# Four engines' order lists rewritten: a GpSimd addition ahead of the W1 load's issue, a ScalarE reciprocal ahead of a relu, and a new order around layer two's last phi(K) tiles

## The chip, the core and the metric

The kernel runs on one core of one Trainium2 chip. A core has five engines that run their own instruction queues in order: TensorE (PE in the profile, with PEld for its weight loads), VectorE (DVE), ScalarE (ACT), GpSimd (POOL) and SyncE (SP, which here only issues DMAs). They meet through semaphores. The metric is the device time of one execution in microseconds (us), the median over several runs; lower is better.

## The reference, cut to what matters

Four residual blocks follow each other on x of 2048 tokens by 512 channels, bf16 in and out: linear attention, MLP, linear attention, MLP. Both layers use the same weights.

```python
def A(x, wqkv, wo):                  # 32 heads of 16 channels
    q, k, v = split(x @ wqkv)
    phi = lambda t: where(t > 0, t + 1, exp(t)) + 1e-6
    pq, pk = phi(q), phi(k)
    kv = einsum("bhsd,bhse->bhde", pk, v)       # sum over all tokens
    z  = einsum("bhsd->bhd", pk)                # sum over all tokens
    o  = (pq @ kv) / ((pq . z) + 1e-6)
    return o @ wo
def B(x, w1, b1, w2, b2):                        # F = 1792
    return gelu(layernorm(x) @ w1 + b1) @ w2 + b2
x = x + A(layernorm(x)); x = x + B(layernorm(x))   # layer one
x = x + A(layernorm(x)); x = x + B(layernorm(x))   # layer two
```

The sums over all tokens in `kv` and `z` are what matters here: no attention output of a layer can be made before the last token tile of that layer has passed through phi(K).

## The kernel before

**Tiles.** Tokens are cut into 16 tiles of 128 (numbered 0 to 15) and four chunks of four tiles (0 to 3). Weights stay in SBUF. In the names, the first number is the layer counted from 0, so `K1_14` is layer two.

**An attention block.** For each token tile the row is normalised (`stats`, `aggr`, `veps`, `pow`, `norm`), transposed (by PE as `PT`, by DMA as `TA`, `TB`) and multiplied with Wk (`K`, L860). `phi` (L823 to 849) then makes phi(K) in three or four instructions: an exponential on ACT (`expk`, L830), a relu on ACT (`reluk`, L841), a minimum on DVE (`mink`, L834 or L843) and the sum on DVE or POOL (`phik`, L847), or instead of relu and sum one fused DVE instruction that reads PSUM (`phik`, L836). Q goes the same way (`Q` L878 or L891, `expq`, `reluq`, `minq`, `phiq`). V is never formed: `G` (L961, L993) accumulates y-transposed times phi(K), and `KV` (L1016) multiplies that with Wv. `z` is summed per chunk by PE (`Z`, L942) or, for the first three chunks of layer two, in fp32 on POOL and DVE (`za`, L914), split in a high and a low half by `zhi` (L920) and `zlo` (L923) and summed over tokens by `ZH` (L930).

**From the sums to the output.** `KV` goes through a mask (`kvm`, L1035) and is multiplied with Wo (`M`, L1039), copied to bf16 (`cpm`, L977 on DVE or L974 on ACT), and used in `WO` (L1109), whose result is added to x (`RA`, L1114). The denominator is made in one of two ways. By channel: `D` (L1085), then ln and exp(-ln) on ACT (`ln` L1087, `rec` L1089) and a product on DVE or POOL (`pr`, L1093). By token: product with a row of z (`pz`, L1061), a sum per head (`red`, L1064), `den` (L1067), `rec` (L1069), `pr` (L1073), and a DMA transpose (`TP`, L1077).

**The MLP.** `W1` (L1141) with gelu on ACT (L1147), `W2` (L1180) with the residual on DVE (`RB`, L1186, L1190). The weights W1 and W2 are loaded in two halves each by DMAs that POOL issues (`w1_0`, `w1_1`, `w2_0`, `w2_1`, L682). Both halves of W1 are needed by every `W1` group.

**What sets the order.** Nothing is searched for when the kernel is built. `CONF["ORDER"]` holds for each engine the full list of its instruction groups by name, written out (from L345 on). `Scheduler.run` (L127) walks the five lists, gives each group its buffers and PSUM banks in the order in which its own estimate reaches them, and `assign_waits` (L283) turns the dependences and the reuse of buffers into semaphore waits. `play` (L1305) emits each list in order. Each engine thus runs its list strictly in order, and a group that waits holds everything behind it on its engine. Which buffer a group gets, and so which earlier group it has to wait for, follows from the lists too: there are four `eb` buffers, four `rb` buffers, eight `pkb` buffers, two `lr` buffers and eight PSUM banks.

```python
            queue = {e: [by_name[n] for n in self.named[e].split()] for e in ENGINES}
...
        G.op("act", lambda e, r=r: e.activation(lr[:, r.slot, :], lr[:, r.slot, :], ACT.Exp, scale=-1.0), 536,
             reads=[f"l{tag}"], writes=[f"l{tag}"], tiles=[r], prio=p, name=f"rec{tag}", lat=110, table="exp")
...
        lambda e, kt=kt, r=r: e.tensor_tensor(yTa(pq)[:, kt, :], yTa(pq)[:, kt, :], lr[:, r.slot, :], op=ALU.mult),
...
        G.op("dve", lambda e: e.tensor_tensor(eb[:, zl.slot, :], zacc[:], dz[:], op=ALU.subtract), 600, reads=["zacc", "dz"],
             writes=["zlo"], tiles=[zl], prio=prio, name=f"zlo{L}", lat=60, fast=True)
```

Of the kernel before, what the change touches and what calls it, by code (L numbers as in the profile page):

```python
# [282 lines left out]
def assign_waits(graph, order, sems, dma_sems):  # L283
# [10 lines left out]
    while len(done) < total:  # L294
        moved = False
        for e in ENGINES:
# [117 lines left out]
        "dve":  # L414
# [962 lines left out]
```

## Time and profile before

| what | value |
|---|---|
| median of 3 runs | 326.38 us (326.32 to 327.12) |
| the profiled execution, its own time | 326.46 us |
| its span, first to last instruction | 324.7 us |
| granted TensorE clock over the span | 1.000 |
| HBM read, written | 8.00 MB, 2.10 MB |

A row of a timeline reads: start in us from the start of the span, length in us, engine, source line, operation, output and inputs by the program's names, shapes, and xN where N like instructions in a row are merged. A bracket at the end says how long the engine had been idle and what ended that. The chain of waits lists what ended last, step by step, backwards from the end, printed in order of time. A 512-column matmul is listed with about 0.38 us, but the next one starts 0.216 us after it, so that starts, not lengths, tell how fast PE goes.

### The profile page before, as it was taken

How to read it: one execution, taken by the hardware profiler on the slowest of the kernel's cores; microseconds unless marked ns; L12 is line 12 of the kernel's file. 1: busy time of each engine (PE TensorE's matmuls, PEld its weight loads, DVE VectorE, ACT ScalarE, POOL GpSimd, SP SyncE). 2: the span in 40 equal slices, each digit the busy share in tenths (PEclk: the TensorE clock that was granted, in tenths of full speed). 3: DMA queues.
4: the chain of work that ended last, by engine and by line, in shares of the span. 5: the costliest groups of instructions: out<-in, count | busy, mean ns of one | idle time of the engine just before them, and what ended most of it. 6: DMA issues, size and time to landing. Idle time of an engine off the chain costs nothing.

```text
span 324.7 us, 4792 instructions
## 1 busy us (share of the span) xinstructions
PE 320.7 (99%) x1729; PEld 158.4 (49%) x1729; DVE 218.6 (67%) x506; ACT 195.2 (60%) x336; POOL 134.9 (42%) x224
## 2 busy tenths in 40 slices
PE   8999999999999999999999999999999999999996
PEld 4444544675444444444444444458644444444443
DVE  5997779999985760213759999999999564000232
ACT  6999698773136129488974567869832543576000
POOL 4673276628803259000266735683541754000000
PEclk9999999999999999999999999999999999999999
DMA  7524558112320205310003200022133123000004
GB/s 241 179 43 89 145 166 296 42 38 49 77 52 5 46 16 91 74 32 2 0 0 68 48 16 2 17 50 50 33 67 81 33 51 81 16 0 2 32 27 153
DMA packets 47028, 20.39 MB, mean 63 GB/s; under 512 B 42076, under 2 KB 45532, under 8 KB 47004
## 3 DMA queue, kind: packets, MB, share of 16 engines
q1 hardware_dynamic: 45532, 15.06, 20.2%
q0 software_dynamic: 1056, 4.72, 4.5%
q10 hardware_dynamic: 416, 0.30, 0.3%
q8 instruction: 14, 0.23, 0.3%
q14 instruction: 10, 0.08, 0.1%
HBM read 8.00 MB, written 2.10 MB: 31 GB/s over the span
## 4 chain that ended last, share of the span: by engine, by line
PE 90%; DVE 6%; ACT 2%; DMA 1%; POOL 0%; issue 0%
PE ps L1141 30%; PE ps L1180 28%; PE ps L1109 9%; PE ps L860 7%; PE ps L878 5%; PE ps L993 3%; PE ps L961 3%; PE ps L891 2%; PE ps L1167 1%; DMA t<-in_A_x_dram 1%; DVE eb L843 1%; DVE gtb L977 1%; DVE gacc L1003 1%; DVE yb L782 1%; PE ps L942 1%; PE ps L805 1%
## 5 line engine op out<-in xcount | busy, mean ns | idle before, releaser
L1147 ACT ACTIVATE gT<-ps,b1c 128x512 bf16<-128x512 f32 (+1 forms) x140 | 77.0, 600 | 63.3 <-PE ps L1141 62.6
L1141 PE MATMUL ps<-t,w 128*128 128x512 bf16 (+1 forms) x560 | 101.4, 336 | 0.0
L1180 PE MATMUL ps<-w,gT 128*128 128x512 bf16 x434 | 98.2, 379 | 0.0
L1141 PEld LDWEIGHTS ps<-t,w 128*128 128x128 bf16 x560 | 54.6, 98 | 43.9 <-ACT t L815 0.3
L1180 PEld LDWEIGHTS ps<-w,gT 128*128 128x128 bf16 x434 | 42.5, 98 | 50.0
L757 POOL TENSOR_TENSOR rstd<-veps,neghalf 128x1 f32<-128x1 f32 x64 | 38.7, 616 | 5.3 <-DVE veps L755 3.1
L830 ACT ACTIVATE eb<-ps 128x512 bf16<-128x512 f32 x56 | 32.6, 600 | 12.4 <-PE ps L860 5.5
L1190 DVE TENSOR_TENSOR pkb<-ps,xsb 128x512 bf16<-128x512 f32 x15 | 10.1, 684 | 40.7 <-PE ps L1180 40.7
L742 DVE BATCH_NORM_STATS2 stats<-xsb 128x6 f32<-128x512 f32 x48 | 32.2, 678 | 0.4
L860 PE MATMUL ps<-wqkv,t 128*128 128x512 bf16 x128 | 31.4, 379 | 0.1
L1109 PE MATMUL ps<-gtb,t 128*128 128x512 bf16 x128 | 30.9, 379 | 0.0
L841 ACT ACTIVATE rb<-ps 128x512 bf16<-128x512 f32 x38 | 22.1, 602 | 8.0 <-PE ps L860 6.6
L747 POOL TENSOR_SCALAR veps<-mv 128x1 f32<-128x1 f32 x32 | 8.7, 271 | 43.8 <-DVE mv L744 40.9
L755 POOL TENSOR_SCALAR veps<-mv 128x1 f32<-128x1 f32 x28 | 7.3, 267 | 45.5 <-DVE mv L744 44.0
L777 ACT ACTIVATE yb<-xsb,nmr,rstd 128x512 bf16<-128x512 f32 x21 | 16.9, 809 | 11.7 <-POOL nmr L774 11.7
L782 DVE TENSOR_SCALAR yb<-xsb,mv,rstd 128x512 bf16<-128x512 f32 x27 | 15.7, 590 | 11.9 <-POOL rstd L757 11.7
L1186 DVE TENSOR_TENSOR xsb<-ps,xsb 128x512 f32<-128x512 f32 x16 | 10.9, 682 | 16.5 <-PE ps L1180 16.5
L843 DVE TENSOR_SCALAR eb<-eb 128x512 bf16<-128x512 bf16 x46 | 14.9, 333 | 7.8 <-ACT eb L830 7.6
L878 PE MATMUL ps<-wqkv,t 128*128 128x512 bf16 x80 | 20.1, 379 | 0.0
L860 PEld LDWEIGHTS ps<-wqkv,t 128*128 128x128 bf16 x128 | 12.2, 98 | 15.0 <-ACT t L815 0.5
L1109 PEld LDWEIGHTS ps<-gtb,t 128*128 128x128 bf16 x128 | 12.3, 97 | 14.3 <-ACT gtb L974 0.5
L1126 POOL TENSOR_TENSOR xsb<-xsb,b2b 128x512 f32<-128x512 f32 x14 | 17.3, 1235 | 1.0 <-DVE yb L782 0.7
(103 smaller groups left out, 395.7 us busy)
## 6 DMA issues: line engine op xcount, KB each, us to landing
w<-in_B_w_dram POOLq DMA_DIRECT2D x4, 896.0 KB, 7.2
out_dram<-pkb SPq DMA_DIRECT2D x15, 128.0 KB, 2.0
t<-in_A_x_dram SPq DMA_DIRECT2D x3, 512.0 KB, 6.9
t<-yb SPq DMA_TRANSPOSE x56, 2.5
wqkv<-in_A_wqkv_dram SPq DMA_DIRECT2D x1, 512.0 KB, 5.3
wqkv<-in_A_wqkv_dram POOLq DMA_DIRECT2D x1, 512.0 KB, 4.4
wo<-in_A_wo_dram POOLq DMA_DIRECT2D x1, 512.0 KB, 5.5
t<-t SPq DMA_TRANSPOSE x20, 2.4
```

Source lines behind the costliest of these rows:

```text
L742: G.op("dve", lambda e: e.bn_stats(stats[:, s.slot, :], src()), 602, reads=src_keys, writes=[k + "s"], tiles=[s, *src_tiles], prio=prio, n ...
L757: G.op("pool", lambda e: e.tensor_tensor(rstd[:, s.slot:s.slot + 1], veps[:, s.slot:s.slot + 1], neghalf[:], op=ALU.pow), 530, reads=[k + ...
L782: G.op("dve", lambda e: e.tensor_scalar(yb[:, y.slot, :], src(), stats[:, s.slot, 2:3] if by_act else mv[:, s.slot, 0:1], rstd[:, s.slot:s ...
L830: G.op("act", lambda e: e.activation(eb[:, et.slot, :], bank(bt), ACT.Exp, scale=factor()), 569 if by else 483, reads=[src_key, *more], wr ...
L841: G.op("act", lambda e: e.activation(rb[:, rt.slot, :], bank(bt), ACT.Relu, scale=factor()), 569 if by else 478, reads=[src_key, *more], w ...
L843: G.op("dve", lambda e: e.tensor_scalar(eb[:, et.slot, :], eb[:, et.slot, :], 1.0, 1e-6, op0=ALU.min, op1=ALU.add), 202, reads=[f"e{tag}"] ...
L860: ins = e.matmul(bank(b), lhsT=yTa(yT)[:, dt, k * P:(k + 1) * P], rhs=wqkv[:, dt, D:2 * D], start=(dt == 0), stop=(dt == DT - 1))
L878: ins = e.matmul(bank(b), lhsT=yTa(yT)[:, dt, k * P:(k + 1) * P], rhs=wqkv[:, dt, 0:D], start=(dt == 0), stop=(dt == DT - 1))
L1109: ins = e.matmul(bank(wb), lhsT=yTa(pq)[:, kt, k * P:(k + 1) * P], rhs=gtb[:, kt, :], start=(kt == 0), stop=(kt == DT - 1))
L1141: ins = e.matmul(bank(b, n), lhsT=w1[:, dt, ft * P:(ft + 1) * P], rhs=yTa(yT)[:, dt, k0 * P:k1 * P], start=(dt == 0), stop=(dt == DT - 1))
L1147: G.op("act", lambda e, ft=ft, b=b, k0=k0, k1=k1, n=n: e.activation(gT[:, g.slot, ft * 512 + k0 * P:ft * 512 + k1 * P], bank(b, n), ACT.Ge ...
L1180: ins = e.matmul(bank(b), lhsT=gT[:, g.slot, ft * 512 + k * P:ft * 512 + (k + 1) * P], rhs=w2[:, ft, :], start=(ft == 0), stop=(ft == FT - 1))
```

## The change

Only the lists in `CONF["ORDER"]` change. PE's list is the same, word for word, and no instruction is added, removed or given to another engine.

Layer one:

- ACT: `rec0_0_3` (the reciprocal of the last of four channel blocks of chunk 0) now stands ahead of `reluq0_1_1`, not behind it.
- POOL: `phiq0_1_1` (a sum of 128x512) now stands ahead of `w1_0`, the DMA issue of one half of W1, not behind it.

Layer two, around the end of phi(K) (tiles 10 to 15) and the first Q tiles:

- ACT: within the 43 places behind `expk1_11`, 34 hold another group than before; among them `expq1_1_2` and `reluq1_1_2` move forward, `expk1_13` and `expk1_15` behind their relus, `reluq1_3_1` ahead of `ln1_0_1`, `expq1_3_0` and `reluq1_2_0` directly behind the three `cpm1` copies.
- DVE: within the 78 places behind `normA1_15`, 59 hold another group than before; `ga1_1_0` and `phiq1_1_2` move ahead of `zhi1`, `mink1_15` directly ahead of it, `minq1_0_1` and `minq1_0_2` behind `phik1_14`, `phiq1_1_3` from ahead of `gt1_0` to between the `kvm1` groups, `minq1_3_1` and `minq1_3_0` far back.
- POOL: `phiq1_3_1` ahead of `pr1_1_0`, `vepsB1_0` ahead of `vepsB1_1`.
- SP: the transposes `TP1_1_2` and `TP1_1_3` change places.

Because the lists change, 43 groups of layer two wait for other groups than before (other `eb`, `rb` buffers and PSUM banks).

```diff
 "act":
-            "reluq0_1_1 rec0_0_3 cpz0 ln0_0_2 rec0_0_2 ...
+            "rec0_0_3 reluq0_1_1 cpz0 ln0_0_2 rec0_0_2 ...
...
-            "reluq1_0_0 expq1_0_0 expq1_1_1 expk1_9 reluk1_8 expk1_8 reluk1_9 normA1_12 reluk1_11 expk1_11 expk1_10 "
-            "reluk1_10 reluq1_1_2 expk1_13 expk1_15 reluk1_13 reluk1_15 expq1_1_2 expk1_12 expk1_14 expq1_0_2 "
-            "expq1_0_1 reluq1_0_3 expq1_0_3 reluq1_0_1 reluq1_0_2 expq1_1_3 cpz1 ln1_0_0 rec1_0_0 reluq1_1_3 "
-            "expq1_3_1 ln1_0_1 rec1_0_1 ln1_0_2 reluq1_3_1 rec1_0_2 expq1_3_0 ln1_0_3 rec1_0_3 cpm1_2 cpm1_1 cpm1_3 "
-            "reluq1_3_0 reluq1_2_1 expq1_2_0 expq1_3_2 reluq1_2_0 reluq1_3_3 expq1_3_3 normB1_1 expq1_2_1 reluq1_3_2 "
+            "reluq1_0_0 expq1_0_0 expq1_1_1 expk1_9 reluk1_8 expk1_8 reluk1_9 normA1_12 reluk1_11 expk1_11 reluq1_1_2 "
+            "expk1_10 expq1_1_2 reluk1_10 reluk1_13 reluk1_15 expk1_13 expk1_15 expk1_12 expq1_0_1 expk1_14 expq1_0_2 "
+            "expq1_0_3 reluq1_0_2 expq1_1_3 reluq1_0_1 reluq1_0_3 cpz1 ln1_0_0 rec1_0_0 reluq1_1_3 reluq1_3_1 ln1_0_1 "
+            "rec1_0_1 ln1_0_2 rec1_0_2 expq1_3_1 reluq1_3_0 ln1_0_3 expq1_2_0 rec1_0_3 cpm1_2 cpm1_1 cpm1_3 expq1_3_0 "
+            "reluq1_2_0 expq1_3_3 reluq1_3_3 normB1_1 expq1_3_2 reluq1_3_2 reluq1_2_1 expq1_2_1 tcB1_0 tcB1_1 "
 "dve":
-            "ga1_0_1 mink1_8 minq1_1_1 normA1_13 phik1_9 ga1_1_1 phiq1_1_1 phik1_8 normA1_15 mink1_11 RB0_14 "
-            "statsA1_14 minq1_0_0 aggrA1_14 mink1_10 phik1_11 phik1_10 normA1_14 ga1_1_3 mink1_15 phiq1_0_0 zhi1 "
-            "minq1_1_2 mink1_13 phiq1_1_2 mink1_12 zlo1 ga1_1_2 phik1_13 ga1_1_0 mink1_14 phik1_12 minq1_0_2 phik1_14 "
-            "minq1_0_1 zsh1 ga1_2_1 zs1_3 minq1_0_3 dz1 zb1 minq1_1_3 phiq1_0_2 phiq1_0_3 phiq1_0_1 gt1_1 ga1_2_2 "
-            "ga1_2_0 red1_1_0 phiq1_1_3 gt1_0 gt1_2 red1_1_1 ga1_2_3 pz1_1_2 gt1_3 minq1_3_1 red1_1_2 kvm1_0 den1_1_1 "
-            "den1_1_0 minq1_3_0 kvm1_1 kvm1_3 kvm1_2 rec1_1_1 cpm1_0 red1_1_3 pr1_1_1 den1_1_2 rec1_1_0 den1_1_3 "
+            "ga1_0_1 mink1_8 minq1_1_1 normA1_13 phik1_9 ga1_1_1 phiq1_1_1 phik1_8 normA1_15 RB0_14 statsA1_14 "
+            "aggrA1_14 minq1_0_0 mink1_11 phik1_11 minq1_1_2 mink1_10 normA1_14 phik1_10 phiq1_0_0 ga1_1_3 phiq1_1_2 "
+            "ga1_1_0 mink1_15 zhi1 mink1_12 zlo1 ga1_1_2 mink1_13 phik1_13 phik1_12 mink1_14 phik1_14 ga1_2_1 zsh1 "
+            "minq1_0_3 minq1_0_1 zs1_3 minq1_0_2 dz1 zb1 phiq1_0_3 phiq1_0_1 minq1_1_3 phiq1_0_2 gt1_1 ga1_2_2 "
+            "red1_1_0 ga1_2_0 gt1_0 gt1_2 red1_1_1 ga1_2_3 den1_1_1 pz1_1_2 gt1_3 red1_1_2 kvm1_2 kvm1_0 den1_1_2 "
+            "phiq1_1_3 kvm1_3 kvm1_1 cpm1_0 den1_1_0 rec1_1_1 red1_1_3 den1_1_3 minq1_3_1 pr1_1_1 rec1_1_0 RA1_0 "
...
 "pool":
-            "... phik0_6 w1_1 phiq0_1_2 wv wo w2_1 w1_0 phiq0_1_1 pr0_0_2 "
+            "... phik0_6 w1_1 phiq0_1_2 wv wo w2_1 phiq0_1_1 w1_0 pr0_0_2 "
...
-            "pr1_0_1 pr1_0_2 pz1_1_3 pr1_0_3 pr1_1_0 phiq1_3_1 pr1_1_2 vepsB1_1 powB1_1 nmrB1_1 vepsB1_0 powB1_0 "
+            "pr1_0_1 pr1_0_2 pz1_1_3 pr1_0_3 phiq1_3_1 pr1_1_0 pr1_1_2 vepsB1_0 vepsB1_1 powB1_1 nmrB1_1 powB1_0 "
 "sp":
-            "... TP1_1_1 TP1_1_0 TP1_1_3 TP1_1_2 TB1_2 TB1_3 "
+            "... TP1_1_1 TP1_1_0 TP1_1_2 TP1_1_3 TB1_2 TB1_3 "
```

30 rows, old and new, of the table ORDER are left out of this document.

## The prediction

> **What bounds the kernel now.** I read the engines' totals first, then the granted clock, then the chain of waits, then the timelines around the places that the lists touch.
>
> ```profile
> PE 320.7 (99%) x1729; PEld 158.4 (49%) x1729; DVE 218.6 (67%) x506; ACT 195.2 (60%) x336; POOL 134.9 (42%) x224
> ...
> PEclk9999999999999999999999999999999999999999
> ...
> PE 90%; DVE 6%; ACT 2%; DMA 1%; POOL 0%; issue 0%
> ```
>
> TensorE is never throttled and holds 90% of the chain. Its list is unchanged, so the change can only shorten or lengthen the moments in which it waits. A busy share of 99% hides these: a matmul's listed length overlaps the next one's. I therefore look for starts that come later than the pace allows. The pace is in the first row below: ten 512-column matmuls from 44.99 to 47.15, or 0.216 us each; a group of four 128-column ones takes 0.22 (48.66 to about 48.88).
>
> ```profile
> 44.99 2.32 PE L961 MATMUL ps<-pkb,yb 128*128 128x512 bf16 x10
> 47.15 0.38 PE L1085 MATMUL ps<-t,zb 128*128 128x512 bf16 x1
> ...
> 48.45 0.38 PE L961 MATMUL ps<-pkb,yb 128*128 128x512 bf16 x1
> 48.66 0.39 PE L1016 MATMUL ps<-gtb,wqkv 128*128 128x128 bf16 x4
> 50.40 0.40 PE L1016 MATMUL ps<-gtb,wqkv 128*128 128x128 bf16 x4 [0.20 <-DVE gtb L977]
> 51.61 1.04 PE L1039 MATMUL ps<-wo,kvb 128*128 128x512 bf16 x4
> ...
> 190.37 1.03 PE L860 MATMUL ps<-wqkv,t 128*128 128x512 bf16 x4
> 191.53 0.18 PE L930 MATMUL ps<-onesm,dz 128*128 128x1 bf16 x1
> 193.47 1.03 PE L878 MATMUL ps<-wqkv,t 128*128 128x512 bf16 x4
> 194.66 0.55 PE L942 MATMUL ps<-onesm,pkb 128*128 128x1 bf16 x16 [0.17 <-DVE pkb L836]
> ```
>
> *Layer one.* Between KV0_0 (48.66) and M0_1 (51.61) PE issues the four KV0 groups (4 x 0.22), two D0_1 matmuls and the four of Q0_2_1 (6 x 0.216): 2.18 us of work in 2.95. PE stands still for 0.77 there, in front of KV0_1 to KV0_3 and M0_1. *Layer two.* K1_14 takes 4 x 0.216 = 0.86 from 190.37, so ZH1 could start at 191.23 and starts at 191.53: 0.30. Q1_1_3 from 193.47 lets Z1_3 start at 194.33; it starts at 194.66: 0.33. Elsewhere in the two regions groups follow at the pace. So the ceiling of any gain is 0.77 + 0.63 = 1.40 us.
>
> The chain says what PE waited for:
>
> ```profile
> 45.12 0.49 ACT rb L841
> 45.60 0.53 ACT lr L1089
> 46.16 1.79 DVE t L1093
> 47.95 2.40 DVE gtb L977 x4
> ...
> 189.91 1.56 DVE eb L923
> ```
>
> In layer one: relu, reciprocal rec0_0_3, product pr0_0_3, then the four copies that feed KV0. In layer two: zlo1 (L923) before ZH1; before Z1_3 it is phik1_14 (L836), by the bracket above.
>
> **The change part by part: layer one.**
>
> ```profile
> 44.58 0.69 DVE L1093 TENSOR_TENSOR t<-t,lr 128x512 bf16<-128x512 bf16 x1 [0.34 <-ACT lr L1089]
> 47.87 2.47 DVE L977 TENSOR_SCALAR gtb<-ps 128x512 bf16<-128x512 f32 x4
> 50.26 0.89 DVE L834 TENSOR_SCALAR eb<-eb 128x512 bf16<-128x512 bf16 x1
> ...
> 188.56 0.42 DVE L920 TENSOR_SCALAR dz<-zacc 128x512 bf16<-128x512 f32 x1
> 189.83 1.64 DVE L923 TENSOR_TENSOR eb<-zacc,dz 128x512 bf16<-128x512 f32 x1
> ```
>
> ```profile
> 44.52 1.67 POOL L682 DMA_DIRECT2D w<-in_B_w_dram  x2
> 46.22 1.17 POOL L847 TENSOR_TENSOR t<-eb,rb 128x512 bf16<-128x512 bf16 x1
> 47.93 1.17 POOL L1093 TENSOR_TENSOR t<-t,lr 128x512 bf16<-128x512 bf16 x1 [0.54 <-ACT lr L1089]
> 49.84 2.40 POOL L1093 TENSOR_TENSOR t<-t,lr 128x512 bf16<-128x512 bf16 x2 [0.75 <-ACT lr L1089]
> ...
> 185.70 2.44 POOL L914 TENSOR_TENSOR zacc<-zacc,pkb 128x512 f32<-128x512 f32 x2
> 189.75 1.17 POOL L847 TENSOR_TENSOR pkb<-eb,rb 128x512 bf16<-128x512 bf16 x1 [1.61 <-DVE t L847]
> ```
>
> The product pr0_0_3 takes 1.79; its like takes 0.69 (44.58). It began at 46.16 and GpSimd's phiq0_1_1 ran from 46.22 to 47.39; the product ended at 47.95, 0.56 after that. So one of two elementwise instructions with operands in SBUF held the other off. The same happened to minq0_2_0 (50.26, 0.89 long) under the product that runs from 49.84 on GpSimd.
>
> The Trainium skill ("SBUF — State Buffer", section "Who interferes with whom") says that VectorE and GpSimd share a port pair as an exclusive lock, and that whichever starts first keeps it. The holding agrees; the order does not, since the product had started 0.06 earlier and lost. By the rule this pair's order would not have needed changing, and layer one's gain would be gone; the row decides.
>
> Now the new order. ScalarE:
>
> ```profile
> 44.45 0.67 ACT L1087 ACTIVATE lr<-ps,eps 128x512 f32<-128x512 f32 x1
> 45.02 0.59 ACT L841 ACTIVATE rb<-ps 128x512 bf16<-128x512 f32 x1
> 46.49 0.70 ACT L1087 ACTIVATE lr<-ps,eps 128x512 f32<-128x512 f32 x1
> 47.22 0.63 ACT L1089 ACTIVATE lr<-lr 128x512 f32<-128x512 f32 x1
> 49.14 0.62 ACT L1089 ACTIVATE lr<-lr 128x512 f32<-128x512 f32 x1
> ```
>
> - A reciprocal behind its own logarithm starts 0.03 after it (46.49 + 0.70, then 47.22), an independent instruction 0.10 before the end of the last (45.02 against 45.12). So rec0_0_3 runs 45.15 to 45.78 instead of ending at 46.13 (45.60 + 0.53), the relu 45.68 to 46.27. What follows on ScalarE is 0.13 later (rec0_0_2 ends near 47.98, not 47.85).
> - pr0_0_3 starts at 45.81 and takes 0.69, to 46.50. phiq0_1_1 now waits for the later relu and starts near 46.32, half a us behind the product, not 0.06: it is GpSimd that waits a little, to about 47.5.
> - Queued behind phiq0_1_1 on GpSimd: the issue of w1_0 (0.74, to 48.25), then pr0_0_2, to 49.43 instead of 49.10. Nobody takes that before the next ln on ScalarE at 49.66. W1 itself is needed 0.77 before today's first W1 matmul, near 60.8.
>
> ```profile
> L682 POOL DMA_DIRECT2D w<-in_B_w_dram x4: 737/946/974, 35.3 to 52.2; - x4
> DMA to landing us min/median/max: 4.4/6.4/8.6
> ```
>
> ```profile
> 61.57 0.38 PE L1141 MATMUL ps<-t,w 128*128 128x256 bf16 x2
> ```
>
> - With the longest landing of those six issues, 8.6, it is there at 47.5 + 8.6 = 56.1: hidden with 4.7 to spare. Without that cover the step would cost its 2.0 us of delay.
> - The copies no longer wait for pr0_0_3 but for their own G0_11 matmuls (last one 48.45 + 0.38 = 48.83). The last starts near 48.98 and, at the row's 2.47 / 4 = 0.62 a copy, ends by 49.65 with 0.05 for the hand-over. KV0_3 at full pace stands at 48.66 + 3 x 0.22 + 2 x 0.216 = 49.75: in time by 0.1.
> - minq0_2_0 then starts near 49.58, 0.26 ahead of GpSimd's product at 49.84 (which hangs on the reciprocal at 49.14 and stays), and takes its plain 0.28. The masks follow KV0_3 at 50.18 and 50.38, M0_1 starts at 50.83. Layer one: 51.61 - 50.83 = 0.78; I take 0.77. Bounds: 0 if minq0_2_0 loses to the product, for then the masks stand where they are; 0.77, since no more standstill is there. I take the far end: two leads of 0.26 and 0.5 against one lost at 0.06.
>
> From there to 182 us every list is as it was, so all of it moves forward together.
>
> **Layer two.** zlo1 shows the same collision: 1.64 from 189.83, beside phik1_15 on GpSimd from 189.75. Like products take 0.69. The latter's start hangs on a PE group (G1_1_2 frees its buffer), so it stays. In the new list zlo1 has only mink1_12 between itself and zhi1, and zhi1 waits for the second of the two zacc sums. These start a little later, since phik1_10 moves behind normA1_14: my estimate is 0.5, which puts the sums' end at 188.6 to 188.9 (188.14 now), zlo1's start at 189.2 to 189.5 (0.42 and 0.28 of work ahead of it), 0.25 to 0.5 ahead of GpSimd, and its end near 190.1. ZH1 is then on time. Behind it six instructions (ga1_1_2 to phik1_14, 2.6 us at today's steps) end near 193.2 because mink1_14 waits for its exponential; Z1_3 wants it at 194.0. If zlo1 loses, it ends at 191.47 as now, 0.30 stays, and the six still end in time for a Z1_3 at 194.33. So the first half gives 0.33 to 0.63; I take 0.63.
>
> The second half has standing room to lose. What PE reads then must also come 0.63 sooner:
>
> ```profile
> 208.72 6.89 SPq L1077 DMA_TRANSPOSE t<-t  x4
> 211.25 1.06 POOL L1073 TENSOR_TENSOR t<-t,rr 128x512 bf16<-128x512 bf16 x1
> 216.49 1.89 PE L1109 MATMUL ps<-gtb,t 128*128 128x512 bf16 x8
> ```
>
> TP1_1_3 now queues on SP behind TP1_1_2. If pr1_1_2 (ending 212.31) moves with PE to 211.7, SP issues at 211.7 and 213.0 (about 1.26 each), and 2.45 later the data is there: 215.4, against WO1_7_0 at 215.87. If pr1_1_2 stays, 216.1: 0.2 lost. phiq1_3_1 in front of pr1_1_0 puts 1.16 ahead of TP1_1_0, which has more room. I charge 0.1 for this half, between 0 and the whole 0.63.
>
> **Sum.** Against the profiled execution (326.46: span 324.7 and 1.76 around it): -0.77 - 0.63 + 0.1 = -1.30, or 325.16. The median shown is 0.08 under that execution: 325.1.
>
> **The rivals.**
>
> 1. *Layer two gives nothing net*: the 0.63 is eaten by WO1_4_0 to WO1_7_0. For it: the many moved groups on a VectorE with hardly an idle row from 180 to 220. Against: transposes still have 0.4. Time 326.38 - 0.77 = 325.6.
> 2. *Layer one gives nothing*: minq0_2_0 or pr0_0_3 still loses to GpSimd. Against: the leads above. Time 326.38 - 0.53 = 325.85; if both parts fail, 326.4.
> 3. *The other side: the W1 issue is held up on GpSimd.* It now falls (47.5 to 48.25) beside the four VectorE copies, and pr0_0_2 waits behind it. Up to 0.5 longer is hidden (ln at 49.66, then ScalarE's slack before the cpm copies); each us beyond moves ScalarE, and so M0 and WO0, by one. Held until the last copy ends (49.65) it takes 2.9, that is 2.15 more and 1.65 on the path: -1.30 + 1.65 = +0.35, or 326.7. It is slower than now from an issue of 2.55 on. Against: the four issues took 0.74 to 0.97, one of them (from 44.52) beside a VectorE product that kept its 0.69.
>
> The Trainium skill ("SBUF — State Buffer", section "SBUF: two separate sides") states such a mechanism: a GpSimd-issued DMA cannot write descriptors while VectorE runs in a mode that takes both ports. The rows show none of it here, though no issue in the trace stands beside copies from PSUM.
>
> **How the numbers follow.** A measurement of this kernel tells about 0.3%, 0.98 us, from no change: under 325.4 is faster, over 327.36 slower. Forecast with its lost race in layer two (324.9 to 325.4): 0.60. Rival 1: 0.18. Rival 2 with both failing: 0.12. Rival 3 and unseen new waits: 0.10, of which 0.06 beyond 327.36. Faster 0.60, same 0.34, slower 0.06. The range 324.8 to 326.5 leaves out more gain than the standstill holds and most of rival 3; the forecast's own is 324.8 to 325.4.
>
> **What would show it.** Right: the L1093 product before the copies at 0.69, M0_1 near 50.8, zlo1 at 0.7 and ZH1 0.86 behind K1_14's start, first W1 matmul near 60.8. Wrong: a 1.6 to 1.8 row on VectorE beside a GpSimd sum, a W1 issue over 1.5, or a bracket <-DMA or <-DVE ahead of L1109 between 205 and 217.

## The result and the profile after

The changed kernel takes 325.48 us (median of 6 runs, 325.25 to 325.92), beside 326.87 us (326.32 to 327.34) of the kernel before in the same comparison: a ratio of 0.9959, 95% interval 0.9945 to 0.9974, or 1.3 us less (1.4 between the medians). The profiled execution took 325.25 us with a span of 323.5; that of before took 326.46 with 324.7.

The view of what TensorE waited for, before and then after (engine and line, the releaser, us in total, times, the longest):

```profile
PE ps L698 <- PEq L1362: 0.8, 1, 0.8
PE ps L1016 <- DVE gtb L977: 0.2, 1, 0.2
PE ps L942 <- DVE pkb L836: 0.2, 1, 0.2
```

```profile
PE ps L698 <- PEq L1362: 0.8, 1, 0.8
```

The two waits of the regions that the lists touch are gone and none has taken their place. The view leaves out waits too short for it; the starts in the timeline of PE give all of it. After:

```profile
48.86 0.39 PE L1016 MATMUL ps<-gtb,wqkv 128*128 128x128 bf16 x4
...
51.05 1.03 PE L1039 MATMUL ps<-wo,kvb 128*128 128x512 bf16 x4
...
189.80 1.03 PE L860 MATMUL ps<-wqkv,t 128*128 128x512 bf16 x4
190.67 0.17 PE L930 MATMUL ps<-onesm,dz 128*128 128x1 bf16 x1
...
192.59 1.03 PE L878 MATMUL ps<-wqkv,t 128*128 128x512 bf16 x4
193.46 0.54 PE L942 MATMUL ps<-onesm,pkb 128*128 128x1 bf16 x16
```

From KV0_0 to M0_1 it is 2.19 us, where before it was 2.95 (48.66 to 51.61): 0.76 less. K1_14 to ZH1 is 0.87 against 1.16, and Q1_1_3 to Z1_3 0.87 against 1.19: 0.29 and 0.32 less. That is 1.37 together. KV0_0 itself starts 0.20 later than before (48.86 against 48.66), which comes from the first 20 us: the order lists of all kernels here are the same up to there, and in their profiles KV0_0 starts anywhere between 48.66 and 49.23; 1.37 - 0.20 is the 1.2 by which the spans differ. (This trace lacks 31 of the 1729 matmul records, so its counts of matmuls are a little low.)

The VectorE and the GpSimd timeline of after at the two places:

```profile
46.01 0.69 DVE L1093 TENSOR_TENSOR t<-t,lr 128x512 bf16<-128x512 bf16 x1 [0.54 <-ACT lr L1089]
47.34 2.53 DVE L977 TENSOR_SCALAR gtb<-ps 128x512 bf16<-128x512 f32 x4 [0.63 <-PE ps L961]
49.79 0.28 DVE L834 TENSOR_SCALAR eb<-eb 128x512 bf16<-128x512 bf16 x1
...
184.78 0.55 DVE L782 TENSOR_SCALAR yb<-xsb,mv,rstd 128x512 bf16<-128x512 f32 x1
188.92 0.68 DVE L923 TENSOR_TENSOR eb<-zacc,dz 128x512 bf16<-128x512 f32 x1
```

```profile
46.55 1.17 POOL L847 TENSOR_TENSOR t<-eb,rb 128x512 bf16<-128x512 bf16 x1 [0.88 <-ACT rb L841]
47.66 0.74 POOL L682 DMA_DIRECT2D w<-in_B_w_dram  x1
50.04 1.17 POOL L1093 TENSOR_TENSOR t<-t,lr 128x512 bf16<-128x512 bf16 x1 [0.45 <-ACT lr L1089]
...
185.74 2.58 POOL L914 TENSOR_TENSOR zacc<-zacc,pkb 128x512 f32<-128x512 f32 x2 [0.99 <-DVE pkb L847]
189.19 1.43 POOL L847 TENSOR_TENSOR pkb<-eb,rb 128x512 bf16<-128x512 bf16 x1 [0.87 <-PE ps L993]
```

The product pr0_0_3 takes 0.69 (1.79 before), 0.54 ahead of phiq0_1_1; the copies then hang on their own matmuls (the bracket names L961) and no longer on the product. zlo1 takes 0.68 (1.64 before), 0.27 ahead of phik1_15, and now it is phik1_15 that is held (1.43 instead of 1.17).

### The profile page after: what moved, and what is told of

Read it like the earlier page. It is cut to its first block, busy times and chain, and to the rows that moved or that the text cites. A ratio compares the mean times of both kernels' runs of the same rounds, so it can differ in the third digit from the quotient of the medians.

```text
span 323.5 us, 4765 instructions
## 1 busy us (share of the span) xinstructions
PE 318.4 (98%) x1698; PEld 159.9 (49%) x1729; DVE 216.5 (67%) x506; ACT 195.0 (60%) x336; POOL 134.8 (42%) x224
## 4 chain that ended last, share of the span: by engine, by line
PE 91%; DVE 7%; issue 1%
PE ps L1180 28%; PE ps L1141 26%; PE ps L860 8%; PE ps L1109 6%; PE ps L878 5%; PE ps L993 4%; PE ps L961 4%; PE ps L891 3%; DVE xsb L1114 2%; DVE stats L742 2%; PE ps L698 2%; DVE yb L782 1%; PE ps L1167 1%; DVE lr L1061 1%; PE ps L1085 1%; DVE rd L1064 1%
## 5 line engine op out<-in xcount | busy, mean ns | idle before, releaser
L1141 PE MATMUL ps<-t,w 128*128 128x512 bf16 (+1 forms) x556 | 101.2, 336 | 0.2
L1141 PEld LDWEIGHTS ps<-t,w 128*128 128x128 bf16 x560 | 54.7, 98 | 43.8 <-ACT t L815 0.3
L860 PE MATMUL ps<-wqkv,t 128*128 128x512 bf16 x125 | 31.1, 379 | 0.2
L1109 PE MATMUL ps<-gtb,t 128*128 128x512 bf16 x123 | 30.1, 379 | 0.3
L782 DVE TENSOR_SCALAR yb<-xsb,mv,rstd 128x512 bf16<-128x512 f32 x27 | 14.8, 559 | 11.4 <-POOL rstd L757 11.2
L878 PE MATMUL ps<-wqkv,t 128*128 128x512 bf16 x76 | 19.4, 379 | 0.2
```

The lines of the kernel that those rows point to most:

```text
L782: G.op("dve", lambda e: e.tensor_scalar(yb[:, y.slot, :], src(), stats[:, s.slot, 2:3] if by_act else mv[:, s.slot, 0:1], rstd[:, s.slot:s ...
L860: ins = e.matmul(bank(b), lhsT=yTa(yT)[:, dt, k * P:(k + 1) * P], rhs=wqkv[:, dt, D:2 * D], start=(dt == 0), stop=(dt == DT - 1))
L878: ins = e.matmul(bank(b), lhsT=yTa(yT)[:, dt, k * P:(k + 1) * P], rhs=wqkv[:, dt, 0:D], start=(dt == 0), stop=(dt == DT - 1))
L1109: ins = e.matmul(bank(wb), lhsT=yTa(pq)[:, kt, k * P:(k + 1) * P], rhs=gtb[:, kt, :], start=(kt == 0), stop=(kt == DT - 1))
L1141: ins = e.matmul(bank(b, n), lhsT=w1[:, dt, ft * P:(ft + 1) * P], rhs=yTa(yT)[:, dt, k0 * P:k1 * P], start=(dt == 0), stop=(dt == DT - 1))
```

## The experiments

Ratios are to the kernel before, run on the same chip beside each group, with 95% intervals. Waits are read from the profile of each run.

### The two layers apart

Layer one's two edits alone:

```diff
 "act":
-            "reluq0_1_1 rec0_0_3 cpz0 ...
+            "rec0_0_3 reluq0_1_1 cpz0 ...
 "pool":
-            "... w2_1 w1_0 phiq0_1_1 pr0_0_2 "
+            "... w2_1 phiq0_1_1 w1_0 pr0_0_2 "
```

> Layer one's two edits alone (rec0_0_3 ahead of reluq0_1_1 on ScalarE, phiq0_1_1 ahead of w1_0 on GpSimd), layer two's lists as before. Port theory: the product pr0_0_3 takes 0.69 instead of 1.79, all four waits of PE between KV0_0 and M0_1 (0.77 us) go, and everything behind moves forward by 0.77: ratio 0.9976 to before. Rival (the early start is used up before the end, at the latest in layer two): the four waits go, but new ones of the same length stand behind them: 1.000.

Measured: 0.9970 (0.9957 to 0.9982). The second kernel is the changed one with just these two edits undone:

> Layer two's lists alone, layer one as before. Port theory: zlo1 takes 0.69 instead of 1.64, ZH1 and Z1_3 lose their waits (0.30 and 0.33), nothing new behind them: 0.63 less, ratio 0.9981. Rival (layer two's many moves are needed only because layer one brings PE forward, or cost as much as they bring): 1.000, with a new wait ahead of M1 or WO1.

Measured: 0.9979 (0.9968 to 0.9991). Both gains exist by themselves and both rivals fall. In the profile of the second, the product of layer one still takes 1.79, and the copies wait for it:

```profile
46.22 1.79 DVE L1093 TENSOR_TENSOR t<-t,lr 128x512 bf16<-128x512 bf16 x1 [0.89 <-ACT lr L1089]
```

### Layer one: either exchange is enough

```diff
 "act":
-            "reluq0_1_1 rec0_0_3 cpz0 ...
+            "rec0_0_3 reluq0_1_1 cpz0 ...
```

> Only the ScalarE exchange of layer one: rec0_0_3 ahead of reluq0_1_1; w1_0 is still issued ahead of phiq0_1_1. Theory 1 (ScalarE's order alone decides): phiq0_1_1 has to wait for its relu until about 46.3 us in any case, so the W1 issue that ends at 46.2 ahead of it costs it nothing; pr0_0_3 runs from 45.8 at 0.69; the whole 0.77 comes: 0.9976. Theory 2 (the GpSimd exchange carries the gain): phiq0_1_1 still holds pr0_0_3 off, which takes over 1.5, and PE waits as before: 1.000.

Measured: 0.9983 (0.9968 to 0.9998).

```diff
 "pool":
-            "... w2_1 w1_0 phiq0_1_1 pr0_0_2 "
+            "... w2_1 phiq0_1_1 w1_0 pr0_0_2 "
```

> Only the GpSimd exchange of layer one: phiq0_1_1 ahead of the issue of w1_0; the relu still runs ahead of the reciprocal. phiq0_1_1 then starts right behind its relu, near 45.7, and ends near 46.9; pr0_0_3 starts at 46.16 and is held off until then: it ends near 47.4 and takes 1.2 to 1.3, not 1.79 and not 0.69. Theory 1 (the copies behind it have 0.6 of room, as their own matmuls end at 47.1 to 48.8): KV0_3 is late by at most 0.2, so 0.55 to 0.75 of the 0.77 comes, 0.9977 to 0.9983, if minq0_2_0 wins against the GpSimd product pr0_1_0, which starts within 0.1 of it; if it loses, the masks stand where they were and 0.1 or less comes, 1.000. Theory 2 (only a product that isn't held off at all helps): 1.000 with the waits at KV0_1 to KV0_3 as before.

Measured: 0.9974 (0.9961 to 0.9987). With ScalarE's exchange alone the product (VectorE, first row) runs at 0.69, ahead of phiq0_1_1 (GpSimd, second row), and PE goes from KV0_0 to M0_1 in 2.19, as in the changed kernel. All four waits go, as Theory 1 has it: the GpSimd exchange adds nothing to it.

```profile
46.02 0.69 DVE L1093 TENSOR_TENSOR t<-t,lr 128x512 bf16<-128x512 bf16 x1 [0.54 <-ACT lr L1089]
46.56 1.16 POOL L847 TENSOR_TENSOR t<-eb,rb 128x512 bf16<-128x512 bf16 x1 [0.16 <-ACT rb L841]
```

With the GpSimd exchange alone, the VectorE and then the GpSimd timeline read:

```profile
46.63 1.23 DVE L1093 TENSOR_TENSOR t<-t,lr 128x512 bf16<-128x512 bf16 x1 [0.89 <-ACT lr L1089]
47.78 2.47 DVE L977 TENSOR_SCALAR gtb<-ps 128x512 bf16<-128x512 f32 x4
50.17 0.28 DVE L834 TENSOR_SCALAR eb<-eb 128x512 bf16<-128x512 bf16 x1
```

```profile
46.16 1.15 POOL L847 TENSOR_TENSOR t<-eb,rb 128x512 bf16<-128x512 bf16 x1 [0.22 <-ACT rb L841]
47.25 0.74 POOL L682 DMA_DIRECT2D w<-in_B_w_dram  x1
50.31 1.17 POOL L1093 TENSOR_TENSOR t<-t,lr 128x512 bf16<-128x512 bf16 x1 [0.74 <-ACT lr L1089]
```

Here phiq0_1_1 comes first, the product is held until it ends (46.16 + 1.15 = 47.31) and ends 0.55 after it, as in the kernel before (0.56). It loses 0.54 instead of 1.10, and that fits into the room that the copies have: PE goes from KV0_0 to M0_1 in 2.27, so 0.68 of the 0.77 come. minq0_2_0 at 50.17 won against the product at 50.31, 0.14 ahead. So the price of a collision is the rest of the other's run less some 0.13 (here 47.31 - 46.63 = 0.68, and 0.54 lost; in the kernel before 47.39 - 46.16 = 1.23, and 1.10 lost), and PE pays only what exceeds the room. The kernel's own estimate in `Scheduler.run` has the same form for the VectorE instructions that it marks `fast` (`dur += max(0.0, pool_busy - at - 130.0)`, in ns).

### A race that the same lists win and lose

The last two kernels and that of layer one alone have layer two's lists exactly as before. In the profile of layer one alone zlo1 loses, as in the kernel before:

```profile
189.30 1.64 DVE L923 TENSOR_TENSOR eb<-zacc,dz 128x512 bf16<-128x512 f32 x1
```

```profile
189.22 1.17 POOL L847 TENSOR_TENSOR pkb<-eb,rb 128x512 bf16<-128x512 bf16 x1 [1.60 <-DVE t L847]
```

and with ScalarE's exchange alone it wins:

```profile
189.28 0.67 DVE L923 TENSOR_TENSOR eb<-zacc,dz 128x512 bf16<-128x512 f32 x1
```

```profile
189.19 1.78 POOL L847 TENSOR_TENSOR pkb<-eb,rb 128x512 bf16<-128x512 bf16 x1 [1.60 <-DVE t L847]
```

zlo1 starts 0.08 behind phik1_15 in the one and 0.09 behind it in the other, which is as near as the records tell, and either may get through. In the second, ZH1 has no wait and Z1_3 starts 0.92 behind Q1_1_3 (1.20 in the first, 0.86 at full pace), with not one edit in layer two; the profiled executions took 325.94 and 325.33. The profile with the GpSimd exchange alone shows a win too (0.68 and 1.78). So the kernel before, which starts the two 0.08 apart (189.83 and 189.75), may lose this race in some executions and win it in others. Its only profile is of a loss, so this is argued from kernels with the same lists, not shown. Its times don't show it either: of the 32 executions that stood beside these four kernels 10 took 325.90 to 326.33 and 22 took 326.53 or more, but in the two comparisons further below only 2 of 21 and 5 of 17 took 326.33 or less, and the kernel of layer two alone, which wins this race with a lead of 0.25, spreads from 325.73 to 326.41 by itself. If it is so, the gain of layer two against the median of before is smaller than the 0.63 of the profile.

### How many of layer two's moves are needed

First, only the part of the lists ahead of `cpz1` (ScalarE) and `zb1` (VectorE) as in the changed kernel, the rest as before:

```diff
 "act":
-            "reluq0_1_1 rec0_0_3 cpz0 ...
+            "rec0_0_3 reluq0_1_1 cpz0 ...
...
-            expk1_11 expk1_10 reluk1_10 reluq1_1_2 ... reluq1_0_2 expq1_1_3 cpz1 ln1_0_0 ...
+            expk1_11 reluq1_1_2 expk1_10 expq1_1_2 ... reluq1_0_1 reluq1_0_3 cpz1 ln1_0_0 ...
 "dve":
-            normA1_15 mink1_11 RB0_14 ... zs1_3 minq1_0_3 dz1 zb1 minq1_1_3 ...
+            normA1_15 RB0_14 statsA1_14 ... zs1_3 minq1_0_2 dz1 zb1 minq1_1_3 ...
```

> The kernel before with the ScalarE list of the change up to cpz1 and its VectorE list up to zb1 (layer one's ScalarE exchange and the first half of layer two's moves); behind these places, and on GpSimd and SyncE, everything as before. Theory 1 (the first half is all that is needed): 0.77 in layer one and 0.63 at ZH1 and Z1_3, nothing lost behind them: ratio 0.9957. Theory 2 (the second half is there for the PSUM banks: with the first half alone the banks are dealt out otherwise, and some six groups of W1 in layer two's first chunk take the bank of the group two places ahead, whose gelu ends 0.7 after its group while PE comes back to the bank after 0.44): about 0.3 lost at each of the six, 1.8 in all: 1.0012, with waits for gelu at W11_0 groups between 219 and 232.

Measured: 1.0039 (1.0027 to 1.0052), slower than before. Then the same lists with the banks held fast:

```diff
+        for w in BANK.split():
+            n, v = w.split(":")
+            for x in v.split(","):
+                i, b = x.split("=")
+                by_name[n].tiles[int(i)].bank = int(b)
...
-            if all(self.state[i] is not None for i in span):
+            if all(self.state[i] is not None for i in span) and getattr(t, "bank", b) == b:
```

`BANK` is a table of the banks that each PE group from K1_10 on has in the kernel before; it moves the line numbers behind it by 32.

> The lists of the run before this one, with every PSUM bank of layer two from K1_10 on fixed as it was in the kernel before. Theory 2 above: the waits at W11_0 are gone, 0.77 + 0.63 come: 0.9957. Theory 3 (VectorE's and GpSimd's old order behind zb1 delays WO1_4 to WO1_7, rival 1 of the prediction): 0.63 is lost again between 205 and 218: 0.9976.

Measured: 0.9964 (0.9951 to 0.9977), 325.20 us in the median, the same as the changed kernel. The first 96 matmuls of W1 in layer two's first chunk in the PE timeline, banks dealt out anew and then banks kept (L1173 is L1141 there):

```profile
217.26 12.46 PE L1141 MATMUL ps<-t,w 128*128 128x256 bf16 x96
```

```profile
217.04 10.64 PE L1173 MATMUL ps<-t,w 128*128 128x256 bf16 x96
```

That is 1.8 us longer. The view of that line's weight loads, banks dealt out anew, says what for:

```profile
L1141 PEld LDWEIGHTS ps<-t,w x112: 95/98/99, 217.0 to 232.3; 128*128 128x128 bf16 x112
...
  ACT gT L1147: 3.0, 8
```

Eight times the loads sat idle for a gelu, 3.0 us; with the banks kept there is no such line. Theory 2 holds in kind and is too small in size: it expected six such waits and 1.8 us, and the medians are 2.5 apart. So nothing behind `cpz1` and `zb1` had to move for VectorE's or GpSimd's sake; those moves matter because the scheduler deals banks out in the order in which its own estimate reaches them.

Next, zlo1 alone moved, two places forward, with banks kept:

```diff
-            "minq1_1_2 mink1_13 phiq1_1_2 mink1_12 zlo1 ga1_1_2 ...
+            "minq1_1_2 phiq1_1_2 zlo1 mink1_13 mink1_12 ga1_1_2 ...
```

> The kernel before with zlo1 two places further ahead in VectorE's list (mink1_13 and mink1_12 behind it), banks fixed as before, layer one as before. zlo1 then starts 0.3 ahead of phik1_15. Theory 1 (only zlo1's own collision costs): zlo1 takes 0.68, both waits go: 0.9981. Theory 2 (the port is what is short: the next VectorE instruction with operands in SBUF, mink1_13, is held in its place until phik1_15 ends, about 1.0 more than its 0.28): ZH1 loses its 0.3, but phik1_14 stays where it was and Z1_3's wait grows to 0.6 to 0.75: 0.999 to 1.000.

Measured: 1.0018 (1.0008 to 1.0028). VectorE, GpSimd and PE in its profile (line numbers 32 higher: L955 is zlo1, L875 mink1_13, L923 Q1_0_3, L910 Q1_1_3, L974 Z1_3):

```profile
189.71 0.69 DVE L955 TENSOR_TENSOR eb<-zacc,dz 128x512 bf16<-128x512 f32 x1
190.32 1.25 DVE L875 TENSOR_SCALAR eb<-eb 128x512 bf16<-128x512 bf16 x1
```

```profile
189.80 1.61 POOL L879 TENSOR_TENSOR pkb<-eb,rb 128x512 bf16<-128x512 bf16 x1 [1.60 <-PE ps L1025]
```

```profile
192.43 1.04 PE L923 MATMUL ps<-t,wqkv 128*128 128x512 bf16 x4
193.36 1.04 PE L910 MATMUL ps<-wqkv,t 128*128 128x512 bf16 x4
194.96 0.55 PE L974 MATMUL ps<-onesm,pkb 128*128 128x1 bf16 x16 [0.56 <-DVE pkb L868]
```

Theory 2 holds: zlo1 is through in 0.69, and mink1_13 behind it is held in its place, 1.25 instead of 0.28. ZH1 gains its 0.30, but Z1_3 starts 1.60 behind Q1_1_3, a wait of 0.74 instead of 0.33, and Q1_0_3 and Q1_1_3 together start 0.15 later than the pace allows: 0.26 more in all, or 1.0008. The lead was 0.09, not the 0.3 expected, since zlo1 takes over the buffer of phiq1_1_2 and starts only when that has ended. The expected 0.999 to 1.000 left the 0.15 out. That the ratio is higher still would fit the race above, if the other side wins it at times; this isn't shown, and 1.0008 is the lower end of the interval.

Last, two VectorE groups moved a few places back, at a place some 6 us ahead of zlo1, and ScalarE's exchange in layer one, with banks dealt out by the lists:

```diff
 "act":
-            "reluq0_1_1 rec0_0_3 cpz0 ...
+            "rec0_0_3 reluq0_1_1 cpz0 ...
 "dve":
-            ... normA1_15 mink1_11 RB0_14 statsA1_14 minq1_0_0 aggrA1_14 mink1_10 ...
+            ... normA1_15 RB0_14 statsA1_14 aggrA1_14 mink1_11 minq1_0_0 mink1_10 ...
```

> The kernel before with three groups moved: rec0_0_3 ahead of reluq0_1_1 on ScalarE, and on VectorE mink1_11 and minq1_0_0 behind aggrA1_14. Nothing else of the change; banks are dealt out by the lists (five groups of layer two wait for others than before). In the trace of before three VectorE instructions ahead of zlo1 are held off too: minq1_0_0 (1.09 instead of 0.28), normA1_14 (1.37 instead of 0.55), mink1_15 (0.64 instead of 0.28). Theory 1 (with the statistics of tile 14 ahead of minq1_0_0, normA1_14 starts about 0.9 earlier, ahead of GpSimd's za1_10, and zlo1 about as much ahead of phik1_15; these collisions are the whole of layer two's gain): 0.77 + 0.58 to 0.63, ratio 0.9957 to 0.9960, zlo1 at 0.68 with a lead of at least 0.3. Theory 2 (the other moves are needed): 0.77 alone, 0.9976, ZH1 and Z1_3 wait as before or a new wait stands at WO1_0.

Measured: 0.9968 (0.9959 to 0.9978), 325.46 us in the median. Its VectorE and GpSimd timelines:

```profile
183.28 1.10 DVE L843 TENSOR_SCALAR eb<-eb 128x512 bf16<-128x512 bf16 x3
185.18 1.41 DVE L782 TENSOR_SCALAR yb<-xsb,mv,rstd 128x512 bf16<-128x512 f32 x1
189.29 0.68 DVE L923 TENSOR_TENSOR eb<-zacc,dz 128x512 bf16<-128x512 f32 x1
```

```profile
185.15 2.45 POOL L914 TENSOR_TENSOR zacc<-zacc,pkb 128x512 f32<-128x512 f32 x2
189.55 1.43 POOL L847 TENSOR_TENSOR pkb<-eb,rb 128x512 bf16<-128x512 bf16 x1 [1.95 <-PE ps L993]
```

Three groups moved give the time of the whole change. Theory 1 is right in the result and wrong in one step: normA1_14 still collides (1.41). It starts 0.4 earlier, not 0.9: 185.18, or 185.39 with the 0.21 that PE is ahead there, against 185.77, just behind the sum za1_10 (185.15). In the changed kernel za1_10 waits for phik1_10, which stands behind normA1_14, and normA1_14 is free. What helps here is that the three minima (mink1_11, minq1_0_0, mink1_10) meet only the end of the sum za1_9, 1.10 together where in the kernel before minq1_0_0 alone took 1.09, and that the statistics no longer wait behind it. That puts zlo1 0.26 ahead of phik1_15, just under the 0.3 expected, and it is enough.

### SyncE's exchange and the load of W1

The changed kernel with SyncE's old order:

```diff
-            ... TP1_1_0 TP1_1_2 TP1_1_3 TB1_2 TB1_3 "
+            ... TP1_1_0 TP1_1_3 TP1_1_2 TB1_2 TB1_3 "
```

> The changed kernel with SyncE's old order, TP1_1_3 ahead of TP1_1_2. pr1_1_3 ends at 212.5 in the changed kernel, 1.6 behind pr1_1_2, so TP1_1_2 is issued at 213.8 instead of 211.2 and lands near 216.3, where WO1_6_0 wants it near 216.1. Theory 1 (the exchange is worth what the order of the two products makes it): 0.1 to 0.3 of wait at WO1_6_0, ratio to before 0.9962 to 0.9968. Theory 2 (the transposes have room in either order): no wait, 0.9959.

Measured: 0.9967 (0.9946 to 0.9987). The interval holds both theories; the trace decides. The last WO1 groups in its PE timeline:

```profile
215.64 2.17 PE L1109 MATMUL ps<-gtb,t 128*128 128x512 bf16 x8
```

The same eight matmuls take 1.89 in the kernel before (216.49): a wait of 0.28 in front of WO1_6_0, as Theory 1 has it. The exchange is needed once PE comes earlier.

The changed kernel with the load of W1 issued later:

```diff
-            ... w2_1 phiq0_1_1 w1_0 pr0_0_2 pr0_1_0 pr0_1_1 w2_0 pr0_1_2 ...
+            ... w2_1 phiq0_1_1 pr0_0_2 pr0_1_0 pr0_1_1 w2_0 w1_0 pr0_1_2 ...
```

> The changed kernel with w1_0 three more places behind, after pr0_1_1 and w2_0. It is issued near 53.4, 5.7 us later than in the changed kernel. The load takes 6.4 to 8.6 from issue to landing, so it lands at 59.8 to 62.0; PE wants it at 61.0. Theory 1 (what hides W1's load is the 5.5 us between its landing at 55.5 and the first W1 matmul): 0 to 1.0 us of wait before the first W1 matmul, ratio to before 0.996 to 0.999. Theory 2 (w2_0, issued just ahead and 896 KB like it, shares the DMA engines and delays the landing by as much again): 3 us or more of wait, 1.005 or more.

Measured: 0.9994 (0.9984 to 1.0004). The weight loads of that time (DMA issue and landing), the transposed tile that the MLP needs first, and PE:

```profile
L682 POOL DMA_DIRECT2D w<-in_B_w_dram x2: 752/856/961, 52.4 to 53.4; - x2
...
DMA to landing us min/median/max: 5.8/7.1/8.3
```

```profile
L792 SPq DMA_TRANSPOSE t<-yb x1: 1205/1205/1205, 58.5 to 58.5; - x1
...
DMA to landing us min/median/max: 3.7/3.7/3.7
```

```profile
60.18 1.04 PE L1109 MATMUL ps<-gtb,t 128*128 128x512 bf16 x4
62.33 0.92 PE L1141 MATMUL ps<-t,w 128*128 128x256 bf16 x7 [1.11 <-DMA t<-yb]
```

PE could have begun W1 at 60.18 + 4 x 0.216 = 61.04 and begins at 62.33: 1.29 lost, near Theory 1 and a little over its 1.0, far from the 3 of Theory 2. The half of W1, issued second, lands at 53.4 + 8.3 = 61.7. What ends the wait is the transposed tile, issued at 58.5 and there at 62.2: it took 3.7, where the changed kernel has 2.4 for the same transfer:

```profile
DMA to landing us min/median/max: 2.4/2.4/2.4
```

The load alone would have cost 0.66 (61.7 against 61.04). That the late load held up a transfer on another queue is read from this one trace, in which the load is what differs and is still in flight at 58.5.

## Why the prediction was right

- *What PE stood still for.* The four waits in layer one and the two in layer two were all there was; the profile after has none of them, 1.37 of the 1.40.
- *Layer one's term, -0.77.* It came, and so did its steps: with 0.20 taken off for the later start, the product at 45.81, phiq0_1_1 at 46.35 (predicted 46.32), the last copy's end at 49.67 (49.65), minq0_2_0 at 49.59 (49.58) with a lead of 0.25, M0_1 at 50.85 (50.83). That ScalarE's exchange alone brings it, and GpSimd's nearly so alone, was not seen: the prediction treated the two as one step.
- *W1's issue.* It took 0.74 at 47.66, beside the first two copies from PSUM: rival 3 has no trace here. That is no test of the rule that the Trainium skill ("SBUF — State Buffer", section "SBUF: two separate sides") was cited for, since no run shows that these copies run in a mode that takes both ports. The load is hidden with some 5 us; the kernel that spends them loses 1.3.
- *Layer two's term, -0.63.* It came (0.61 by the starts). The end of the sums was right: 188.32 after, or 188.89 on before's clock, which is 0.57 later there (0.77 less 0.20), at the late end of 188.6 to 188.9. So zlo1's lead of 0.27 is at the low end of 0.25 to 0.5. What was overlooked is how VectorE gets there. These rows of the kernel before stand ahead of zlo1:

```profile
183.28 1.09 DVE L843 TENSOR_SCALAR eb<-eb 128x512 bf16<-128x512 bf16 x1
185.77 1.37 DVE L782 TENSOR_SCALAR yb<-xsb,mv,rstd 128x512 bf16<-128x512 f32 x1 [0.46 <-POOL rstd L757]
187.66 0.64 DVE L843 TENSOR_SCALAR eb<-eb 128x512 bf16<-128x512 bf16 x1
```

  They are minq1_0_0, normA1_14 and mink1_15, held off like zlo1: 2.0 us above their plain 0.28, 0.55 (184.78 after) and 0.28, twice what zlo1 loses. Two moves that take most of the wait from the first of them are enough.
- *The 0.1 charged for the second half.* Nothing was lost there: the changed kernel has no wait at WO1. The transposes follow at the times worked out, and the exchange on SyncE is worth 0.28. The reason given for the moved groups behind Z1_3, VectorE's and GpSimd's work, was not the one that counts; that is the banks, 2.5 us, of which the prediction says nothing.
- *The races.* "Two leads of 0.26 and 0.5 against one lost at 0.06" held, and 0.14 was won too. What failed is the picture of a fixed outcome: zlo1's collision was taken as a property of the lists, while at such a distance the same lists lost it in two profiles and won it in two. In the pairs shown here that start 0.14 or more apart the earlier one always won, which agrees with the rule of the Trainium skill ("SBUF — State Buffer", section "Who interferes with whom") that issue order decides. For those within 0.1 the starts in the rows do not tell the winner: the product 0.06 ahead lost, zlo1 0.08 to 0.09 behind lost twice and won twice. So the lost pair from which the prediction read that the order does not agree was too close to tell.
- *The size.* -1.30 was forecast and 1.3 measured; PE gained 1.37 at the places named, and the 0.1 charged for the second half was not spent. The time is 325.5 and not 325.1 because the runs of before in the comparison have a median of 326.87, where the forecast started from 326.38.

## What to carry to other kernels

Where VectorE and GpSimd both work on operands in SBUF, read the listed length of each against its plain length: an instruction at two or three times its like has been held off, and its cost on the path is about the rest of the other's run less the room behind it. A lead of a quarter of a microsecond, from whatever move is cheapest, was enough in every pair here. Leads under 0.1 us were no order at all: the same lists won and lost, so that an edit elsewhere can seem to have won the race by itself. Where buffers are dealt out by a scheduler's estimate, hold them fast before judging a change of order, for the order itself may be sound and the new banks cost more than it brings.

## What the runs showed that was not expected

- The same pair of instructions, at the same distance within 0.01 us, blocked the one or the other in the profiles of kernels with the same lists there (1.64 and 1.17, or 0.67 and 1.78).
- When the holder of the way ends, the next one that is waiting pays: with zlo1 through first, phik1_15 is held for 0.4 and then holds mink1_13 for 1.0.
- With a weight load of 896 KB that GpSimd issued still in flight, a DMA transpose from SyncE's queue took 1.3 us longer (3.7 against 2.4 from issue to landing, in one trace each).
